# The router's exponential takes its input from SBUF, and a batch's last logits move to the next head pair

## The chip, the cores and the metric

The program runs on one core of one Trainium2 chip. A core has five engines that run side by side and meet only at semaphores: TensorE (PE, matmuls and transposes, results into PSUM), VectorE (DVE), ScalarE (ACT), GpSimd (POOL) and SyncE (SP, which issues most transfers). Each engine takes its instructions strictly in the order of its own list. The metric is the time of one execution on the device in microseconds; a lower number is better.

## The reference

Two parts follow each other. Causal attention with a decay, for 8 batches, 8 heads, 576 positions and a head size of 64:

```python
scores = scale * np.matmul(q, k.transpose(0, 1, 3, 2))
decay = cum[:, :, :, None] - cum[:, :, None, :]      # cum: running sum of log(f)
scores = np.where(causal, -1000000000.0, scores + decay)
attn = softmax(scores)                               # rows divided by their sum + 1e-9
x = (attn @ v) as 4608 rows of 512
```

Then a mixture of experts over these 4608 rows. Each row goes to one of 8 experts, the one with the largest logit, and its result is weighted with that expert's probability:

```python
logits = x @ w_gate                                  # 4608 x 8
expert_idx = np.argmax(logits, axis=1)
probs = np.exp(logits - logits.max(-1, keepdims=True))
probs /= probs.sum(-1, keepdims=True) + 1e-09
gate_w = probs[np.arange(N), expert_idx]
h = np.maximum(xe @ w1[e], 0.0); out[mask] = gate_w[mask, None] * (h @ w2[e])
```

The change touches only how `logits`, `logits - max` and `exp` are scheduled and where they are stored.

## The kernel before

**Attention.** The work goes head pair by head pair: 32 pairs n, four for each batch (p is n modulo 4), each in seven steps i from 0 to 6. In a step, PE computes a group of score tiles of pair n into one of three PSUM banks (pool `ps_s`, L332) and transposes a group of the weights of pair n-1 into one of two banks (`ps_t`, L400, L419, L430). DVE adds the mask and takes the row's extreme in the same instruction (`s_red`, L339, followed by a short read of the accumulator); ACT takes the exponential (L346) and copies most of the transposed tiles to SBUF (L391), DVE the rest (L389). In step 1, PE also does all of attention-times-values of pair n-2 (`av`, L470) into the two banks of pools `ps_v` and `ps_m`, ACT casts keys for pair n+1 (`k_first`, L291) and then copies the two results to SBUF (`av_out`, L479). POOL prepares the operands of later pairs (L249, L287, L296).

**Routing.** When the fourth pair of batch b has gone through `av`, which is step 1 of pair g = 4b+6, the routing of that batch is spread over the following pairs by a table (`r` in `fin_tasks`) of entries (pair after g, step, function). Right behind `av` of pair g stand four small matmuls for the gate (`fin_gate`, L542). In pair g (p = 2) follow a transpose of the output (`fx[0]`, L508) in step 2, the logits of four row blocks (`lg[0]`) in step 3 and of the fifth (`lg[1]`) in step 4: PE transposes (L558), DVE multiplies by the reciprocal row sums (L562), and after the last block DVE adds over the heads (L568). In pair g+1 (p = 3) stand `softmax` and `expert` in step 1, `rank` in step 3; in pair g+2 (p = 0) `gate` and `slot`, and so on. The bank of `lg` is `fin_bank[0]`, which alternates between `ps_v` in even and `ps_m` in odd steps. For the last batch (b = 7) the order is another one, written out in `Moe.finish`.

`softmax` takes the maximum of the logits (L805) and subtracts it (L807, into `w.sh`). `expert` takes the exponential on ACT (L811) and then, on DVE, finds the index of the largest logit (L814 to L824); `rank` counts with six small matmuls on PE (L840, L842) which need the result of L824, and DVE finishes the count (L847 to L856).

**One PSUM bank for the routing.** `c.ps_r` is a single bank of 512 columns that all the routing's small PSUM values share: the logits in columns 0 to 39, `w.sh` in 40 to 79, the one-hot rows, the counts. The framework adds a semaphore wait where two engines use this bank, also where both only read it.

**What sets the order.** Each engine's order is the order of the code, pinned step by step (`InOrder.pin`); nothing reorders it. The framework adds the waits. After the attention the experts follow one by one (L1093 for the first, L1116 for the second matrix), and their first expert's work already begins in the last pairs.

Of the kernel before, what the change touches and what calls it, by code (L numbers as in the profile page):

```python
# [8 lines left out]
F32 = mybir.dt.float32  # L9
# [4 lines left out]
AF = mybir.ActivationFunctionType  # L14
ALU = mybir.AluOpType
# [4 lines left out]
P = 128  # L20
# [61 lines left out]
def psum(pool):  # L82
    return pool.tile([P, 512], F32, name="ps", tag="ps")
# [11 lines left out]
def attention_all(c, tc, qkT, va, vb, f, wgd, x_dram, batch_done, more_consts, extra):  # L95
# [6 lines left out]
    nc = tc.nc  # L102
    V = nc.vector
# [11 lines left out]
    with ExitStack() as st:  # L115
# [5 lines left out]
        ps_s, ps_t, ps_v, ps_m = c.ps_s, c.ps_t, c.ps_v, c.ps_m  # L121
# [4 lines left out]
        def note(r):  # L126

            pe_last[:] = [r.ins]
            return r
# [416 lines left out]
                    ))  # L546
                nc.scalar.copy(gT[:, q0:q1], g[:, 0 : q1 - q0])

        def fin_logits(b, part):
            rinv = rinvs[b]  # L550
            if part == 0:
                lgs[b] = (c.ps_r[:, 0:40].rearrange("p (t e) -> p t e", e=8),
                          sm.tile([P, 5, 8, 8], F32, name="gq", bufs=1))
            lg, gq = lgs[b]
            pg = psum(fin_bank[0])
            tiles = (0, 1, 2, 3) if part == 0 else (4,)
            for i, t in enumerate(tiles):
                note(nc.tensor.transpose(  # L558
                    pg[:, P * i : P * i + P], gT[:, P * t : P * t + P], c.ident
                ))  # L560
            for i, t in enumerate(tiles):
                V.tensor_tensor(  # L562
                    gq[:, t],
                    pg[:, P * i : P * i + P].rearrange("q (h e) -> q e h", e=16)[:, 0:8, :],
                    rinv[:, t, :].unsqueeze(1).to_broadcast([P, 8, 8]), ALU.mult,
                )
            if part == 1:
                V.tensor_reduce(lg, gq, AX.X, ALU.add)  # L568


        fin_bank = [ps_m]

        def fin_tasks(b):

            (softmax, expert, gate, rank, slot, hi, lo, table), after = batch_done(
                b, lambda: lgs[b][0]
            )
            fx = [lambda t=t: fin_x(b, t, b == B - 1 and t > 0) for t in range(5)]  # L580
            lg = [lambda p=p: fin_logits(b, p) for p in range(2)]
            g = NPAIR * b + 6
            if b == B - 1:
                return dict(fx=fx, lg=lg, softmax=softmax, expert=expert, gate=gate,
                            rank=rank, slot=slot, hi=hi, lo=lo, table=table,
                            logits=lambda: fin_gate(b))
            r = [(0, 2, fx[0]), (0, 3, lg[0]), (0, 4, lg[1]), (1, 1, softmax),
                 (1, 1, expert), (1, 3, rank)]
            if b < B - 2:
                r += [(2, 1, gate), (2, 1, slot), (2, 2, fx[1]), (2, 3, fx[2]),  # L590
                      (3, 1, hi), (3, 1, lo), (3, 2, fx[3]), (3, 3, fx[4]), (3, 5, table)]
            else:
                r += [(2, 1, gate), (2, 1, slot), (2, 2, fx[1]), (2, 3, hi), (2, 3, lo),
                      (2, 4, fx[2]), (2, 5, fx[3]), (2, 6, fx[4]), (3, 0, table)]
            for dn, i, f in r + after:
                tasks.setdefault((g + dn, i), []).append(f)
# [47 lines left out]
        for n in range(NP + 2):  # L644
            b, p = divmod(n, NPAIR)
# [84 lines left out]
E = 8  # L730
# [56 lines left out]
def route_stages(c, tc, b, lg_of, last):  # L787

    nc = tc.nc
    V = nc.vector  # L790
    rs = c.rps
    bc = lambda a: a.unsqueeze(2).to_broadcast([P, 5, E])
    flat = lambda a: a.rearrange("p t e -> p (t e)")
    w = Ctx()
    vl = c.vals[:, 5 * b : 5 * b + 5, :]

    part = lambda o, n: c.ps_r[:, o : o + n]
    tokens = lambda o, n: part(o, n * E).rearrange("p (t e) -> p t e", e=E)  # L800

    def softmax():
        lg = lg_of()
        mx = rs.tile([P, 5], F32, name="mx")
        V.tensor_reduce(mx, lg, AX.X, ALU.max)  # L805
        w.sh = tokens(40, 5)
        V.tensor_tensor(w.sh, lg, bc(mx), ALU.subtract)  # L807

    def expert():
        w.ex = rs.tile([P, 5, E], F32, name="ex")  # L810
        nc.scalar.activation(w.ex, w.sh, AF.Exp)  # L811

        cand = rs.tile([P, 5, E], F32, name="cand")
        V.scalar_tensor_tensor(  # L814
            flat(cand), flat(w.sh), 0.0, flat(c.iota5m), ALU.is_ge, ALU.mult
        )
        w.ei = part(128, 5)
        V.tensor_reduce(w.ei, cand, AX.X, ALU.min)
        w.oh = tokens(80, 6)
        V.tensor_tensor(w.oh[:, 0:5], bc(w.ei), c.iota5m, ALU.is_equal)  # L820
        V.memset(w.oh[64:128, 4, :], 0.0)
        V.memset(w.oh[:, 5, :], 0.0)
        w.ohb = rs.tile([P, 6, E], BF16, name="ohb")
        V.tensor_copy(w.ohb, w.oh)  # L824

    def gate():

        gw = part(136, 5)
        V.tensor_reduce(gw, w.ex, AX.X, ALU.add)
        V.tensor_scalar(gw, gw, 1.0e-9, None, ALU.add)  # L830
        V.reciprocal(gw, gw)
        for i in range(3):
            V.tensor_copy(vl[:, :, 3 + i], gw)
            if i < 2:
                V.tensor_tensor(gw, gw, vl[:, :, 3 + i], ALU.subtract)

    def rank():

        w.pr = part(192, 48)
        nc.tensor.matmul(w.pr[:, 0:48], c.trib, flat(w.ohb), start=True, stop=False)  # L840
        for s in range(1, 6):
            nc.tensor.matmul(  # L842
                w.pr[:, 8 * s : 48], c.onesb, flat(w.ohb[:, 0 : 6 - s]),
                start=False, stop=(s == 5),
            )
        rk = rs.tile([P, 6, E], F32, name="rk", bufs=2)
        V.tensor_tensor(rk, w.pr[:, 0:48].rearrange("p (t e) -> p t e", e=E),  # L847
                        c.carry.unsqueeze(1).to_broadcast([P, 6, E]), ALU.add)
        c.carry = rk[:, 5, :]
        V.tensor_tensor(rk[:, 0:5], w.oh[:, 0:5], rk[:, 0:5], ALU.mult)  # L850
        w.r = rs.tile([P, 5], F32, name="r")
        w.rp = part(144, 5)
        for r in (w.r, w.rp):
            V.tensor_reduce(r, rk[:, 0:5], AX.X, ALU.add)

        V.memset(w.ei[64:128, 4:5], -4.0 - E)  # L856

    def slot():
        r, ei = w.r, w.ei
        V.scalar_tensor_tensor(c.key[:, 5 * b : 5 * b + 5], ei, 8192.0, r,  # L860
                               ALU.mult, ALU.add)

        th = rs.tile([P, 5, NST - 1], F32, name="th")
        V.tensor_tensor(
            th, w.rp.unsqueeze(2).to_broadcast([P, 5, NST - 1]),
            c.iotaP[:, 1:NST].unsqueeze(1).to_broadcast([P, 5, NST - 1]), ALU.is_ge,
        )
        hi = rs.tile([P, 5], F32, name="hi")
        V.tensor_reduce(hi, th, AX.X, ALU.add)
        w.lo = part(152, 5)  # L870
        V.scalar_tensor_tensor(w.lo, hi, -float(P), w.rp, ALU.mult, ALU.add)
        w.hi = part(160, 5)
        V.scalar_tensor_tensor(w.hi, ei, float(NST), hi, ALU.mult, ALU.add)

    def onehot_hi():
        eqh = rs.tile([P, 5, NHI], BF16, name="eqh")
        V.tensor_tensor(
            eqh, w.hi.unsqueeze(2).to_broadcast([P, 5, NHI]),
            c.iotah.unsqueeze(1).to_broadcast([P, 5, NHI]), ALU.is_equal,
        )  # L880
        w.R = rs.tile([P, 5, 6, NHI], BF16, name="Rr")
        eng = V if last else nc.gpsimd
        for t in range(5):
            eng.tensor_tensor(
                w.R[:, t], eqh[:, t].unsqueeze(1).to_broadcast([P, 6, NHI]),
                vl[:, t].unsqueeze(2).to_broadcast([P, 6, NHI]), ALU.mult,
            )

    def onehot_lo():
        w.A = rs.tile([P, 5, P], BF16, name="Ar")  # L890
        V.tensor_tensor(w.A, w.lo.unsqueeze(2).to_broadcast([P, 5, P]),
                        c.iota128.unsqueeze(1).to_broadcast([P, 5, P]), ALU.is_equal)

    def table():

        pt = part(256, 6 * NHI)
        for t in range(5):
            nc.tensor.matmul(pt[:, 0 : 6 * NHI], w.A[:, t],
                             w.R[:, t].rearrange("p v h -> p (v h)"),
                             start=(t == 0), stop=(t == 4))  # L900
        tab = c.tab.rearrange("p v h -> p (v h)")
        V.tensor_tensor(tab, tab, pt[:, 0 : 6 * NHI], ALU.add)

    return [softmax, expert, gate, rank, slot, onehot_hi, onehot_lo, table]


# [514 lines left out]
```

## Time and profile before

| | us |
|---|---|
| median of 3 runs | 862.28 (861.4 to 862.44) |
| the profiled execution | 861.09 |
| its span, first to last instruction | 859.3 |
| PE busy in the span | 816.6 (95%) |
| DVE, ACT, POOL busy | 462.9, 432.3, 388.2 |

The profiled execution is 1.19 us shorter than the median, and 1.8 us of it lie outside the span. In the timeline, times count from the start of the span; a row gives the start, the length, the engine, the line, the operation, what it writes and reads, the size and, in square brackets, how long the engine stood idle before it and who ended that. A matmul's row is as long as its way through the array, so rows of PE overlap; how long PE needs for a group is seen from one start to the next.

### The profile page before, as it was taken

To read this page: it belongs to the slowest core of one execution; us is meant where nothing else is said; L and a number is where in the kernel's file an instruction comes from. 1 tells how busy PE (TensorE), PEld (TensorE's weight loads), DVE (VectorE), ACT (ScalarE), POOL (GpSimd) and SP (SyncE) were. 2 spreads that over 40 slices of the span, in tenths; PEclk is the share of its full clock that TensorE was granted. 3 is DMA by queue.
4 is the path that set the end of the run, shared out by engine and by line. 5 is a ranking of instruction groups with operands and counts; after the bars stand their busy time and mean duration, and the time that the engine had idled before them with its cause. 6 is when DMAs were issued, how large, how long until landed. Compare 5 with 4: busy or idle time off the path is not lost. (4 is left out here: it accounts for less than half of the span.)

```text
span 859.3 us, 15386 instructions
## 1 busy us (share of the span) xinstructions
PE 816.6 (95%) x5664; PEld 713.9 (83%) x5664; DVE 462.9 (54%) x1427; ACT 432.3 (50%) x1108; POOL 388.2 (45%) x310
## 2 busy tenths in 40 slices
PE   4899999999999999999999999999999999999992
PEld 3778787878787878788899899898898998988982
DVE  7656767676767778655472544445425444354200
ACT  6888888888888989855221223122122221231210
POOL 7798696969696978651530230312203103101010
PEclk9999999999999999999999999999999999999996
DMA  7997676767676765522651450533415405324000
GB/s 170 223 191 162 163 178 164 183 150 187 152 184 154 176 152 146 175 93 86 191 190 50 147 170 21 189 109 119 149 46 171 143 4 183 104 74 132 1 37 17
DMA packets 39893, 114.65 MB, mean 133 GB/s; under 512 B 6847, under 2 KB 8895, under 8 KB 36104
## 3 DMA queue, kind: packets, MB, share of 16 engines
q1 hardware_dynamic: 32776, 93.70, 42.2%
q0 software_dynamic: 6400, 19.93, 6.4%
q8 instruction: 46, 0.75, 0.4%
q14 instruction: 31, 0.25, 0.1%
q10 hardware_dynamic: 640, 0.01, 0.0%
HBM read 94.07 MB, written 20.55 MB: 133 GB/s over the span
## 5 line engine op out<-in xcount | busy, mean ns | idle before, releaser
L1116 PE MATMUL ps<-w,hh 128*128 128x512 f32 x640 | 199.3, 395 | 0.0
L346 ACT ACTIVATE sc<-sc,nmx 128x512 f32<-128x512 f32 (+4 forms) x288 | 167.3, 582 | 34.7 <-DVE nmx L339 34.2
L1124 POOL DMA_INDIRECT out<-y,si_fast x37 | 42.4, 1146 | 312.1 <-ACT y L1123 283.4
L339 DVE CUSTOM_DVE_ANT_0 sc<-ps,mask 128x512 f32<-128x512 f32 (+4 forms) x288 | 129.2, 479 | 63.7 <-PE ps L332 63.0
L1098 ACT ACTIVATE hh<-ps 128x384 fp32r<-128x384 f32 (+1 forms) x128 | 56.1, 438 | 194.5 <-PE ps L1093 194.5
L1093 PE MATMUL ps<-xa,w 128*128 128x384 f32 x768 | 145.1, 337 | 0.1
L332 PE MATMUL ps<-qk 128*128 128x288 f32 (+4 forms) x384 | 126.9, 361 | 16.0 <-ACT qk L271 10.8
L1099 DVE SCALAR_TENSOR_TENSOR hl<-ps,hh 128x384 fp32r<-128x384 f32 (+1 forms) x128 | 62.4, 489 | 146.2 <-ACT hh L1098 145.0
L1116 PEld LDWEIGHTS ps<-w,hh 128*128 128x128 f32 x640 | 118.2, 188 | 23.6
L1093 PEld LDWEIGHTS ps<-xa,w 128*128 128x128 f32 x768 | 132.7, 188 | 1.4 <-DVE hl L1099 0.2
L1116 PE MATMUL ps<-w,hl 128*128 128x512 f32 x320 | 124.8, 395 | 0.0
L332 PE MATMUL ps<-k,q 68*128 68x288 f32 (+4 forms) x384 | 105.7, 323 | 5.2 <-POOL k L249 3.8
L249 POOL TENSOR_TENSOR k<-raw,qk 64x1152 fp32r<-64x1152 f32 x30 | 79.4, 2647 | 53.7 <-ACT qk L291 49.0
L1093 PE MATMUL ps<-xb,w 128*128 128x256 f32 x768 | 101.8, 283 | 0.0
L1093 PEld LDWEIGHTS ps<-xb,w 128*128 128x128 f32 x768 | 98.9, 189 | 2.8
L470 PE MATMUL ps<-aT,va_t 128*64 128x256 f32 (+3 forms) x896 | 94.6, 354 | 0.0
L1123 ACT ACTIVATE y<-ps,g_fast 128x512 f32<-128x512 f32 x37 | 25.5, 689 | 136.6 <-PE ps L1116 130.7
L391 ACT COPY aT<-ps 128x512 f32<-128x512 f32 (+1 forms) x156 | 83.2, 534 | 14.1 <-PE ps L400 6.8
L332 PEld LDWEIGHTS ps<-qk 128*128 128x128 f32 x384 | 69.6, 195 | 23.6 <-ACT qk L271 10.8
L249 POOL TENSOR_TENSOR qk<-raw,qk 64x1280 fp32r<-64x1280 f32 x30 | 87.8, 2928 | 2.4
L470 PEld LDWEIGHTS ps<-aT,va_t 128*64 128x64 f32 x896 | 58.9, 137 | 29.2 <-issue 6.1
L969 DVE CAST w<-wraw 128x1024 fp32r<-128x1024 f32 x56 | 39.2, 707 | 80.3 <-PE ps L1116 54.3
(161 smaller groups left out, 1133.2 us busy)
## 6 DMA issues: line engine op xcount, KB each, us to landing
raw<-in_qkT SPq DMA_DIRECT2D x58, 608.0 KB
wraw<-in_w SPq DMA_DIRECT2D x63, 512.0 KB
va_t<-in_va SPq DMA_DIRECT2D x32, 256.0 KB
x_dram<-row SPq DMA_DIRECT2D x32, 256.0 KB
raw<-in_qkT SPq DMA_DIRECT2D x6, 320.0 KB
raw<-in_qkT SPq DMA_DIRECT2D x6, 288.0 KB
vb<-in_vb SPq DMA_DIRECT2D x32, 32.0 KB
x_dram<-row SPq DMA_DIRECT2D x8, 128.0 KB
```

The lines of the kernel that those rows point to most:

```text
L249: return eng.tensor_tensor(o, raws[n][p0 : p0 + 64, c0:c1], ops[n][0][p0 : p0 + 64, c0:c1].bitcast(F32), ALU.subtract,)
L332: note(nc.tensor.matmul(out, ql[:, q0 : q0 + P], kl[:, j, k0 : k0 + kw], start=(i == 0), stop=(i == last),))
L339: V.tensor_tensor_reduce(scs[n][:, dst : dst + src.shape[1]], src, m, -0.125, init, ALU.add, ALU.min, nms[n][:, col : col + 1],)
L346: nc.scalar.activation(x, x, AF.Exp, bias=nms[n][:, col : col + 1], scale=-1.0, accum_out=acc)
L391: nc.scalar.copy(dst, src)
L470: c.last_av = note(nc.tensor.matmul(pv[j * HD : (j + 1) * HD, q0 - qa : qb - qa], l, r, start=(blk == 0), stop=(blk == nb - 1),))
L969: V.tensor_copy(w[:, 0], raw)
L1093: c.note(nc.tensor.matmul(ph[:, 0:n], w[:, wi, fs], x[:, xi, kt, :], start=(k == 0), stop=(k == 3 * KT - 1),))
L1098: nc.scalar.activation(hh[:, ft, :], ph[:, 0:n], AF.Relu)
L1099: nc.vector.scalar_tensor_tensor(hl[:, ft, :], ph[:, 0:n], 0.0, hh[:, ft, :].bitcast(F32), ALU.max, ALU.subtract,)
L1116: c.note(nc.tensor.matmul(py, hi_[:, ft, ms], w[:, wi], start=(ft + k == 0), stop=(ft == FT - 1 and k == 2),))
L1124: nc.gpsimd.indirect_dma_start(out=self.out, out_offset=bass.IndirectOffsetOnAxis(ap=si[:, s : s + 1], axis=0), in_=y, in_offset=None, bou ...
```

## The change

There are two edits, in the table of `fin_tasks` and in `softmax`/`expert`.

- `lg[1]`, the logits of a batch's fifth row block, leaves step 4 of pair g and stands in step 0 of pair g+1, and it uses the bank of `ps_m` instead of the one that `fin_bank` names (which is `ps_v` in both steps).
- `softmax` subtracts the maximum a second time, into a new SBUF tile `shs`, and the exponential reads `shs` instead of `w.sh`. DVE's search for the largest logit goes on reading `w.sh`.

The last batch goes through `Moe.finish`, where the place and the bank of `lg[1]` stay as they were; there the second subtraction alone is new.

```diff
-        def fin_logits(b, part):
+        def fin_logits(b, part, bank=None):
...
-            pg = psum(fin_bank[0])
+            pg = psum(bank or fin_bank[0])
...
-            r = [(0, 2, fx[0]), (0, 3, lg[0]), (0, 4, lg[1]), (1, 1, softmax),
+            r = [(0, 2, fx[0]), (0, 3, lg[0]), (1, 0, lambda: fin_logits(b, 1, ps_m)), (1, 1, softmax),
                  (1, 1, expert), (1, 3, rank)]
...
         w.sh = tokens(40, 5)
         V.tensor_tensor(w.sh, lg, bc(mx), ALU.subtract)
 
+        w.shs = rs.tile([P, 5, E], F32, name="shs")
+        V.tensor_tensor(w.shs, lg, bc(mx), ALU.subtract)
+
     def expert():
         w.ex = rs.tile([P, 5, E], F32, name="ex")
-        nc.scalar.activation(w.ex, w.sh, AF.Exp)
+        nc.scalar.activation(w.ex, w.shs, AF.Exp)
```

From L808 on the lines of the changed kernel count three higher (L814 becomes L817, L840 becomes L843).

DVE before, around step 4 of pair g (`sc`, `nmx` are the scores and their row extremes, `pr` the routing's bank, `gq` the logits per head; the bracket names the engine whose semaphore is waited for):

```order
L389 COPY aT<-ps 128x2x2x128 [waits PE_49]
L562 TENSOR_TENSOR gq<-ps,rinv 128x64 [waits PE_49]
L568 TENSOR_REDUCE pr<-gq 128x40 [waits DVE_49]
L339 ISA sc,nmx<-ps,mask 128x288 [waits PE_49]
L339 ISA nmx 128x1
L389 COPY aT<-ps 68x2x64
```

and from `softmax` on, some rows further down:

```order
L805 TENSOR_REDUCE mx<-pr 128x5
L807 TENSOR_TENSOR pr<-pr,mx 128x40 [waits DVE_49]
L814 SCALAR_TENSOR_TENSOR cand<-pr,iota5m 128x40 [waits Activation_49]
L818 TENSOR_REDUCE pr<-cand 128x5 [waits DVE_49]
L820 TENSOR_TENSOR pr<-pr,iota5m 128x40 [waits DVE_49]
```

The search (`cand`) waits for ACT, though it takes nothing from it. The same engine in the changed kernel, from step 0 of pair g+1:

```order
L339 ISA sc,nmx<-ps,mask 128x512 [waits PE_49]
L339 ISA nmx 128x1
L562 TENSOR_TENSOR gq<-ps,rinv 128x64 [waits PE_49]
L568 TENSOR_REDUCE pr<-gq 128x40 [waits DVE_49]
L339 ISA sc,nmx<-ps,mask 128x512 [waits PE_49]
L339 ISA nmx 128x1
L805 TENSOR_REDUCE mx<-pr 128x5 [waits DVE_49]
L807 TENSOR_TENSOR pr<-pr,mx 128x40 [waits DVE_49]
L810 TENSOR_TENSOR shs<-pr,mx 128x40 [waits DVE_49]
L817 SCALAR_TENSOR_TENSOR cand<-pr,iota5m 128x40
L821 TENSOR_REDUCE pr<-cand 128x5 [waits DVE_49]
L823 TENSOR_TENSOR pr<-pr,iota5m 128x40 [waits DVE_49]
```

The two instructions of `lg[1]` now stand behind the reductions of two joint tiles and of step 0, there is one more subtraction (L810), and `cand` has lost its wait for ACT. On ACT the exponential keeps its place and its wait for DVE; only its source is another.

PE in the changed kernel, from step 0 of pair g+1 into its `av`, the transpose of `lg[1]` (L558) now behind the first transposes:

```order
L332 MATMUL ps<-k_1_145,q_1_143 128x512 [waits DMAHW2_49,DMAHW1_49,Pool_49]
L400 MATMUL ps<-ident,sc 128x128 [waits DVE_49]
L400 MATMUL ps<-ident,sc 128x128 x3
L558 MATMUL ps<-ident,gT 128x128
L332 MATMUL ps<-qk_920 128x512 [waits DVE_49,PE_49]
```

and some rows on, the second half of `av`, which writes the bank of `ps_m`:

```order
L470 MATMUL ps<-aT,vb_176 64x64 [waits DMAHW0_49]
L470 MATMUL ps<-aT,vb_176 64x64
L470 MATMUL ps<-aT,va_t 64x320 [waits DVE_49]
L470 MATMUL ps<-aT,va_t 64x320
L470 MATMUL ps<-aT,va_t 64x192 x2
L470 MATMUL ps<-aT,va_t 64x64 x2
```

Before, L558 stood behind the transposes of step 4 of pair g, and the first `64x320` had no wait; now it waits until DVE has read the logits out of that bank (L562).

## The prediction

> **What bounds the kernel now.** I read the waits of the whole span first, then the span cut at the starts of the head pairs, then the timelines of PE, DVE and ACT in one pair. The waits have one entry at the place of the change, DVE's search for the largest logit behind ACT's exponential: 24.5 us in 8 times.
>
> ```profile
> DVE cand L814 <- ACT ex L811: 24.5, 8, 3.5
> ```
>
> DVE is no bound by its busy time, so this matters only if PE waits for DVE later. The cut says so. A row gives the stretch, its length, then busy time of PE, PEld, DVE, ACT and POOL. The first row is a pair with p = 3, where the search and the count (`rank`) stand; the second a pair with p = 1, in which PE has eight more full transposes and five small matmuls (the table):
>
> ```profile
> 128.10:139.85 11.75, 10.50 (x90) 8.36 (x89) 7.42 (x38) 8.90 (x26) 7.89 (x5) 1.00 0.57 134
> 150.40:161.19 10.79, 10.79 (x97) 9.46 (x96) 8.13 (x31) 9.78 (x28) 10.58 (x12) 1.00 0.79 190
> ```
>
> The pair with less work for PE takes 0.96 us longer. PE is the bound in the second pair; in the first it stands still. Where, the starts on PE's timeline tell, p = 3 first, p = 1 as the measure behind it:
>
> ```profile
> 128.65 0.60 PE L400 MATMUL ps<-ident,sc 128*128 128x128 f32 x4
> 129.33 0.47 PE L332 MATMUL ps<-qk 128*128 128x512 f32 x1
> 130.41 1.84 PE L470 MATMUL ps<-aT,va_t 128*64 128x256 f32 x16
> 133.27 0.44 PE L332 MATMUL ps<-qk 128*128 128x384 f32 x1
> 133.91 0.63 PE L400 MATMUL ps<-ident,sc 128*128 128x128 f32 x4
> 134.90 0.62 PE L400 MATMUL ps<-ident,sc 128*128 128x128 f32 x4
> 135.97 0.20 PE L840 MATMUL pr<-ohb,trib 128*128 128x48 bf16 x1 [0.44 <-DVE ohb L824]
> 136.13 0.36 PE L332 MATMUL ps<-qk 128*128 128x256 f32 x1
> 136.85 0.66 PE L419 MATMUL ps<-ident,sc 128*128 128x128 f32 x4
> 138.53 0.60 PE L430 MATMUL ps<-ident,sc 128*128 128x128 f32 x4
> 139.85 0.47 PE L332 MATMUL ps<-qk 128*128 128x512 f32 x1 [0.72 <-DVE nmx L339]
> 141.03 0.47 PE L332 MATMUL ps<-qk 128*128 128x512 f32 x1
> ```
>
> ```profile
> 150.40 0.48 PE L332 MATMUL ps<-qk 128*128 128x512 f32 x1
> 150.95 0.60 PE L400 MATMUL ps<-ident,sc 128*128 128x128 f32 x4
> 151.31 0.48 PE L332 MATMUL ps<-qk 128*128 128x512 f32 x1
> 157.31 0.63 PE L400 MATMUL ps<-ident,sc 128*128 128x128 f32 x4
> 157.77 0.60 PE L508 MATMUL ps<-ident,xT 128*64 128x128 f32 x4
> 158.13 0.37 PE L332 MATMUL ps<-qk 128*128 128x256 f32 x1
> 158.70 0.61 PE L419 MATMUL ps<-ident,sc 128*128 128x128 f32 x4
> ```
>
> Four transposes take 0.36 us to the next scores (150.95 to 151.31) and 0.46 to an operation of another kind (157.31 to 157.77). In p = 3 the same steps take 0.68, 1.07 (134.90 to 135.97) and 1.32 us (138.53 to 139.85): 0.32, 0.61 and 0.96 us of standing still. With the 0.15 by which step 4's scores take longer (136.13 to 136.85 against 158.13 to 158.70) that is 2.04 us. DVE's and ACT's timelines of the same pair show the source:
>
> ```profile
> 127.88 0.22 DVE L562 TENSOR_TENSOR gq<-ps,rinv 128x64 f32<-128x64 f32 x1
> 128.53 0.45 DVE L339 CUSTOM_DVE_ANT_0 sc<-ps,mask 128x288 f32<-128x288 f32 x1
> 129.57 0.69 DVE L339 CUSTOM_DVE_ANT_0 sc<-ps,mask 128x512 f32<-128x512 f32 x1
> 131.03 0.21 DVE L807 TENSOR_TENSOR pr<-pr,mx 128x40 f32<-128x40 f32 x1
> 134.71 0.20 DVE L814 SCALAR_TENSOR_TENSOR cand<-pr,iota5m 128x40 f32<-128x40 f32 x1 [3.47 <-ACT ex L811]
> 135.70 0.21 DVE L824 CAST ohb<-pr 128x48 bf16<-128x48 f32 x1
> 137.91 0.29 DVE L389 COPY aT<-ps 128x128 f32<-128x128 f32 x1 [0.43 <-ACT aT L391]
> ```
>
> ```profile
> 136.42 0.62 ACT L346 ACTIVATE sc<-sc,nmx 128x384 f32<-128x384 f32 x1 [1.37 <-DVE nmx L339]
> 137.42 0.46 ACT L391 COPY aT<-ps 128x384 f32<-128x384 f32 x1
> 137.78 0.62 ACT L346 ACTIVATE sc<-sc,nmx 128x384 f32<-128x384 f32 x1
> ```
>
> The exponential stands on ACT behind the key cast and the copies of `av`'s results, so it comes late, and DVE, whose L807 is done at 131.24, stands behind it for 3.47 us. Step 2's reduction is late by that, ACT waits 1.37 us for it, ACT's copy of step 3 (137.42) is late, DVE's copy of the same bank (137.91) waits for that one, and behind it stand the end of the count and step 4's reduction, which frees the bank that PE needs at 139.85 (its row names L339's `nmx`).
>
> **The change part by part.** *The search no longer waits for ACT.* DVE then goes from L807 (131.03) to the second subtraction at 131.26 and to the search at 131.49, 3.22 us earlier, and the one-hot row (L824) is there at 135.91 - 3.22 = 132.69, before PE reaches the count. The 0.61 us are gone. Step 2's reduction is no longer behind anything on DVE; it waits for PE.
>
> *The second subtraction.* It reads a PSUM operand and a small SBUF operand and writes SBUF, like L562, and has the size of L807 (0.21 us). With L562 as the nearest row of that kind, and free of dependence on what POOL does at the time in 40 instances, I take 0.23 us from start to start:
>
> ```profile
> L562 DVE TENSOR_TENSOR gq<-ps,rinv x40: 211/215/219, 81.5 to 395.6; 128x64 f32<-128x64 f32 x40
> ```
>
> The bounds are 0.2 and 0.25 us. What hides it: DVE is through at 132.69 and has no scores before about 133.8. Without that cover it would cost 0.23 us in each of 7 batches, 1.6 us. The exponential now waits for this subtraction (131.47), which is long done when ACT comes to it; its length changes by nothing that matters, since nobody on DVE waits for it until the next pair.
>
> *The logits of the fifth block.* L562 and L568 leave DVE between 127.88 and 128.53, so 0.65 us come off ahead of the last reductions of pair g, which is why PE's second scores came 0.32 us late (129.33): that goes too. The 0.65 us stand in step 0 now, ahead of step 1's reduction, whose scores PE has by then; that one ends near 130.9, and ACT needs it after 131. On PE, L558 goes from one pair to the next. As its price I take the 0.46 - 0.36 = 0.10 us by which an operation of another kind comes later behind four transposes, with 0 below and above it the 0.36 us of a whole group of four. It falls off pair g and comes onto pair g+1, so the sum does not hang on it. No transfer is moved, and no other queue is passed.
>
> *The new wait of `av`.* PE's 64x320 matmuls now wait for L562. DVE's reduction of step 0 moves from 129.57 to 128.92 and ends 0.61 later (its accumulator is read at its end), so L562 ends near 129.8. PE comes to the matmuls behind the first half of `av`, which starts at 130.19 and takes some 1.8 us: near 132.0. The cover is 2.2 us; behind the wait stands all of PE.
>
> *What is late next.* PE without standing still: first scores 128.10, the second 0.91 later as in p = 1 and 0.10 for L558 (129.11), then the distances of the rows, 130.41 - 129.33 = 1.08 and 133.27 - 130.41 = 2.86: step 2 at 133.05, its transposes 0.64 later at 133.69, done 0.62 later at 134.31. ACT copies them at 134.35, needs 0.36 until the exponential (137.42 to 137.78): 134.71 in place of 136.42. That is 1.71 us earlier, and this shift passes through ACT's copy of step 3 and DVE's copy (137.91, now 136.20) to the reduction of step 4 and to PE at 139.85, now 138.14. PE itself, without the 2.04 and with the 0.10, would be there at 137.91, so 0.23 us of its standing still remain: DVE's tail, the copy, the count and the reduction in a row, still sets the end. Pair g+1 shrinks by 1.71 to 10.04 us, pair g by 0.10. The next pair keeps its length, because the same tail comes before it. 1.81 us for each of the six batches with a whole next pair: 10.9 us.
>
> *The seventh batch.* The last pair of scores (batch 6) has the same wait, and there PE stands still longer:
>
> ```profile
> 357.34 0.62 PE L400 MATMUL ps<-ident,sc 128*128 128x128 f32 x4
> 359.74 0.62 ACT L346 ACTIVATE sc<-sc,nmx 128x384 f32<-128x384 f32 x1 [1.26 <-DVE nmx L339]
> 361.71 0.29 DVE L389 COPY aT<-ps 128x128 f32<-128x128 f32 x1 [0.91 <-ACT aT L391]
> 364.76 1.00 PE L400 MATMUL ps<-ident,sc 128*128 128x128 f32 x4 [1.94 <-DVE aT L389]
> ```
>
> By the same walk PE's transposes of step 2 come 0.3 us earlier, are done at 357.66, and the exponential starts at 358.07 in place of 359.74: 1.67 us, which run through 361.71 to 364.76. With pair g's 0.10 these are 1.8 us. The eighth batch's wait is the small rest of the 24.5 us, in a stretch where PE has the experts' work, and counts nothing.
>
> *The clock.* Behind that pause the granted clock falls to half for 3.4 us; the column before the last two is the clock:
>
> ```profile
> 136.40:139.80 3.40, 2.73 (x21) 2.27 (x20) 2.86 (x18) 2.86 (x10) 3.32 (x3) 1.00 0.03 8
> 361.60:365.00 3.40, 1.46 (x12) 1.22 (x11) 3.18 (x15) 2.28 (x10) 0.00 (x0) 0.99 0.12 46
> 365.00:368.40 3.40, 3.40 (x20) 2.51 (x20) 1.40 (x6) 2.69 (x7) 0.00 (x0) 0.51 0.03 7
> ```
>
> A stretch in which PE was busy for 1.46 of 3.40 us preceded the fall, one with 2.73 did not cause it. DVE frees PE 1.67 us earlier, PE itself is there some 0.8 us earlier (0.3 at the second scores, the rest at the count), so about 1.1 us of pause and 2.3 busy remain, nearer to the first row. I count the fall as gone. Half of 3.4 us is 1.7 us of lost work, but the copies and splits behind which PE stands there are not faster, so I take 0.4, with 0 and 1.7 as bounds. [...] The trace has the fall directly behind the pause, and I go by it.
>
> The sum is 10.9 + 1.8 + 0.4 = 13.1 us. The profiled execution of 861.09 us (859.3 of span and 1.8 around it) becomes 848.0; the median, 1.19 above it, becomes 862.28 - 13.1 = 849.2 us. Behind 400 us PE has no pause to speak of, so nothing gives the gain back.
>
> **The rivals.** *The tail keeps its place (15%).* Only what comes ahead of the count goes, 0.32 and 0.61, and the end of p = 3 stays as late because ACT is the one that is late there. For: ACT is busy 8.90 us of that pair, the most after PE. Against: it waited 1.37 us for DVE. 7 times 0.93 is 6.5, so 855.8 us.
>
> *All of PE's pauses go (10%).* 2.04 us and the 0.27 that p = 0 loses in the same way at its second scores (139.85 to 141.03 is 1.18, where p = 1 has 0.91), in six batches; 1.94 + 0.3 + 0.1 in the seventh; and the clock's 1.7: 17.9 us, 844.4. Against: the walk leaves 0.23 us in each p = 3, and the 0.27 behind it.
>
> *DVE's wait is hidden (3%).* Then nothing changes: 862 us. PE's own rows name DVE as what ended its pauses, which speaks against it.
>
> *Slower: `av` waits for the logits (3%).* If DVE came to L562 late, PE would stand at the 64x320 matmuls with everything behind it. It decides from 2.2 us of lateness on, and from about 4.0 (2.2 and the 1.81 of gain) the kernel is slower. Were the 3.47 us to stand ahead of L562 and the rest of the gain lost, it would cost 1.27 us in 7 batches, 8.9 us: 871. DVE waits for nothing of ACT between 127.88 and 131.03.
>
> **How the numbers follow.** The forecast, with 69%, has 849.2 us. The range from 844.9 to 855.2 reaches towards the second rival and the first as far as partial forms of them go, and leaves out their ends and the last two. Faster by over 0.2% (1.7 us, about what runs of this kernel can tell) are the forecast and the first two rivals, 94%; 3% each for no change and slower.
>
> **What would show it.** The entry of `cand` behind the exponential is gone from the waits, p = 3 takes about 10.0 us instead of 11.75, p = 0 and p = 1 stay at 10.55 and 10.8, p = 2 loses 0.1; PE's pause at the count is gone, and the one at the end of the pair is 0.2 us instead of 0.96. No row shows 64x320 behind L562. Wrong would be a pair p = 3 above 10.8, a `cand` that still waits, or a clock at half behind the last pair of scores, which alone costs 0.4.

## The result and the profile after

The changed kernel takes 848.72 us (median of 4 runs, 847.09 to 849.95) against 862.31 before; the ratio is 0.9843, with a 95% interval from 0.9823 to 0.9864. 849.2 was forecast. The profiled execution takes 849.63 us, 847.9 of them span.

DVE's search for the largest logit, now L817, no longer waits for anybody: its entry under the waits is gone, and its own line has no idle time before it. What is left near it is a single wait of ACT for the second subtraction, of the last batch; before, ACT waited there in the same way for the first one (2.3 us). From the view of that line and from the waits of the whole span, after:

```profile
L817 DVE SCALAR_TENSOR_TENSOR cand<-pr,iota5m x8: 189/190/191, 88.6 to 385.2; 128x40 f32<-128x40 f32 x8
```

```profile
ACT ex L814 <- DVE shs L810: 2.5, 1, 2.5
```

The span cut at the starts of the head pairs, with the columns as before: p = 3, p = 0, p = 1 and p = 2.

```profile
127.96:138.03 10.07, 10.00 (x91) 8.49 (x90) 7.82 (x40) 9.05 (x27) 6.79 (x5) 1.00 0.68 155
138.03:148.58 10.55, 10.54 (x90) 8.95 (x90) 9.38 (x42) 9.86 (x29) 8.02 (x5) 1.00 0.77 188
148.58:159.39 10.81, 10.81 (x98) 9.50 (x96) 8.29 (x31) 9.78 (x28) 10.60 (x12) 1.00 0.79 192
159.39:170.76 11.37, 11.37 (x109) 9.40 (x106) 6.74 (x31) 10.08 (x28) 10.03 (x6) 1.00 0.70 164
```

The pair with the search and the count has gone from 11.75 to 10.07 us. The pairs with p = 0 and p = 1 are as they were. PE's timeline of p = 3, to be read against that of before:

```profile
128.51 0.60 PE L400 MATMUL ps<-ident,sc 128*128 128x128 f32 x4
128.95 0.27 PE L558 MATMUL ps<-ident,gT 128*128 128x128 f32 x1
128.98 0.48 PE L332 MATMUL ps<-qk 128*128 128x512 f32 x1
...
133.56 0.63 PE L400 MATMUL ps<-ident,sc 128*128 128x128 f32 x4
...
134.56 0.62 PE L400 MATMUL ps<-ident,sc 128*128 128x128 f32 x4
135.02 0.19 PE L843 MATMUL pr<-ohb,trib 128*128 128x48 bf16 x1
...
135.17 0.37 PE L332 MATMUL ps<-qk 128*128 128x256 f32 x1
...
135.74 0.60 PE L419 MATMUL ps<-ident,sc 128*128 128x128 f32 x4
...
137.36 0.60 PE L430 MATMUL ps<-ident,sc 128*128 128x128 f32 x4
138.03 0.47 PE L332 MATMUL ps<-qk 128*128 128x512 f32 x1
```

The second scores follow 0.47 us behind the first transposes, with the moved L558 between (0.68 before, without it). The count follows 0.46 us behind the transposes of step 3 (1.07 before), the next pair 0.67 us behind the last transposes (1.32 before, 0.36 where nothing waits). Step 4's scores take 0.57 us (135.17 to 135.74), as in p = 1, and no longer 0.72. DVE in the same pair, and two rows of ACT:

```profile
131.00 0.21 DVE L807 TENSOR_TENSOR pr<-pr,mx 128x40 f32<-128x40 f32 x1
131.25 0.20 DVE L810 TENSOR_TENSOR shs<-pr,mx 128x40 f32<-128x40 f32 x1
131.36 0.19 DVE L817 SCALAR_TENSOR_TENSOR cand<-pr,iota5m 128x40 f32<-128x40 f32 x1
...
132.35 0.21 DVE L827 CAST ohb<-pr 128x48 bf16<-128x48 f32 x1
133.76 0.56 DVE L339 CUSTOM_DVE_ANT_0 sc<-ps,mask 128x384 f32<-128x384 f32 x1 [1.21 <-PE ps L332]
...
136.09 0.29 DVE L389 COPY aT<-ps 128x128 f32<-128x128 f32 x1 [0.38 <-ACT aT L391]
136.30 0.20 DVE L850 TENSOR_TENSOR rk<-pr,rk 128x48 f32<-128x48 f32 x1
...
137.11 0.42 DVE L339 CUSTOM_DVE_ANT_0 sc<-ps,mask 128x256 f32<-128x256 f32 x1
```

```profile
133.78 0.25 ACT L814 ACTIVATE ex<-shs 128x40 f32<-128x40 f32 x1
...
134.60 0.62 ACT L346 ACTIVATE sc<-sc,nmx 128x384 f32<-128x384 f32 x1
```

The exponential keeps its place on ACT, 5.82 us after the start of the pair (6.36 before), but DVE is through at 132.56 and waits for PE for 1.21 us. The order of the tail is the old one: copy of step 3, end of the count, reduction of step 4.

Where the time went, in three stretches of the span: up to the start of pair 5, the last one ahead of the first routing; from there to the start of pair 31, the last with scores; and from there to the end. Before:

```profile
0.00:62.13 62.13, 44.80 (x317) 38.10 (x317) 39.09 (x131) 47.37 (x119) 51.02 (x60) 1.00 0.88 198
62.13:351.44 289.31, 281.64 (x2445) 235.24 (x2444) 205.92 (x893) 252.81 (x699) 229.69 (x156) 1.00 0.69 164
351.44:859.30 507.86, 490.13 (x2908) 440.52 (x2906) 217.83 (x405) 132.14 (x292) 107.53 (x96) 0.98 0.33 108
```

and after:

```profile
0.00:64.13 64.13, 48.09 (x317) 40.40 (x317) 39.43 (x131) 47.89 (x121) 49.73 (x59) 0.95 0.86 193
64.13:342.05 277.92, 277.49 (x2446) 235.55 (x2444) 207.14 (x899) 253.04 (x698) 231.31 (x157) 1.00 0.72 171
342.05:847.90 505.85, 487.99 (x2909) 439.45 (x2907) 218.56 (x408) 131.97 (x292) 107.77 (x96) 0.99 0.34 108
```

The middle gives 11.39 us and the end 2.01, together 13.40; the start, in which no changed instruction stands, takes 2.00 us more in this execution, at a mean clock of 0.95 instead of 1.00 (the last section). So the two profiled executions differ by 11.46 us, and without their starts by 13.40, close to the 13.6 between the medians.

### The profile page after: what moved, and what is told of

Read it like the earlier page. It is cut to its first block, busy times and chain, and to the rows that moved or that the text cites. A ratio compares the mean times of both kernels' runs of the same rounds, so it can differ in the third digit from the quotient of the medians.

```text
span 847.9 us, 15394 instructions
## 1 busy us (share of the span) xinstructions
PE 813.6 (96%) x5664; PEld 715.4 (84%) x5664; DVE 465.1 (55%) x1435; ACT 432.9 (51%) x1108; POOL 388.8 (46%) x310
```

## The experiments

The theory was the one of the prediction: DVE's wait at the search makes its tail late, the tail frees the bank that PE waits for, and the place of the fifth block's logits costs the second scores. Each kernel below was timed in three rounds beside the kernel before. The length of the pairs with p = 3 and p = 0 is read from PE's timeline as above, as the median over the steady batches.

**One edit alone.** The exponential reads from SBUF and the logits stay:

```diff
-            r = [(0, 2, fx[0]), (0, 3, lg[0]), (1, 0, lambda: fin_logits(b, 1, ps_m)), (1, 1, softmax),
+            r = [(0, 2, fx[0]), (0, 3, lg[0]), (0, 4, lg[1]), (1, 1, softmax),
```

> Only the exponential reads from SBUF; the fifth block's logits stay in step 4 of pair g. Theory (DVE's wait at the search made the tail of p = 3 late; the logits' place costs the second scores): the search has no wait for ACT, the pause at the count is gone, but PE's second scores in p = 3 stay 0.3 us late, so step 2's exponential starts 1.5 us earlier instead of 1.7; p = 3 takes 10.25 us, p = 2 stays at 11.49, and six batches with 1.5, 1.5 for the seventh and 0.4 for the clock give about 851.5 us. Rival (the logits' place is the larger part): p = 3 above 11 us, 857 or more.

850.27 us, ratio 0.9863 (0.9846 to 0.9879). p = 3 takes 10.31 us, p = 2 11.48, the count follows 0.46 us behind its transposes, and PE's second scores come 0.70 us behind the first ones, as late as before:

```profile
127.28 0.60 PE L400 MATMUL ps<-ident,sc 128*128 128x128 f32 x4
127.98 0.47 PE L332 MATMUL ps<-qk 128*128 128x512 f32 x1
```

The theory holds, the rival does not.

And the logits move, while the exponential goes on reading the bank:

```diff
-        w.shs = rs.tile([P, 5, E], F32, name="shs")
-        V.tensor_tensor(w.shs, lg, bc(mx), ALU.subtract)
...
-        nc.scalar.activation(w.ex, w.shs, AF.Exp)
+        nc.scalar.activation(w.ex, w.sh, AF.Exp)
```

> Only the fifth block's logits move; the exponential still reads the PSUM bank. Theory: the search still waits for ACT, some 20 us in 8 times; the second scores' 0.32 us are gone, ACT gets its joint tile 0.65 us earlier and so reaches the exponential up to 0.65 us earlier, p = 3 takes 11.1 us, p = 2 11.38, about 857 us. Rival (the logits' place is the larger part): p = 3 near 10.1 us, 849 to 851.

857.36 us, ratio 0.9943 (0.9927 to 0.996); p = 3 takes 11.22 us, p = 2 11.38. The waits of DVE from 70 us on, and PE's way to the count:

```profile
DVE cand L814 <- ACT ex L811: 20.0, 8, 2.8
```

```profile
134.52 0.62 PE L400 MATMUL ps<-ident,sc 128*128 128x128 f32 x4
135.28 0.20 PE L840 MATMUL pr<-ohb,trib 128*128 128x48 bf16 x1
```

The wait shrinks from 24.5 to 20.0 us, as expected: ACT's exponential now stands 5.82 us after the start of the pair. The second scores are on time (0.47 us), of the 0.61 us at the count 0.30 are left (0.76 us against 0.46), and the pause at the end of the pair keeps its length (1.33 us). Against 862.43 us alone, the edits are worth 12.2 and 5.1 us; together 13.6, measured against 862.31. They overlap: an earlier ACT shortens the same wait that the first edit removes.

**The wait without SBUF.** The logits moved, no second subtraction, and the exponential put behind the search in the program:

```diff
     def expert():
-        w.ex = rs.tile([P, 5, E], F32, name="ex")
-        nc.scalar.activation(w.ex, w.shs, AF.Exp)
...
         V.tensor_copy(w.ohb, w.oh)
+        w.ex = rs.tile([P, 5, E], F32, name="ex")
+        nc.scalar.activation(w.ex, w.sh, AF.Exp)
```

> The logits moved as in the change, no second subtraction; the exponential reads the PSUM bank, but stands behind the search in the program, so that the bank's wait falls on ACT (for the end of the search) and not on DVE. Theory (it is the order of two readers of one bank, not where the input lies): as the change, 848.7 within 1.5 us, p = 3 at 10.07 us, the search without a wait. Rival (reading from SBUF itself is worth something, or ACT now waits for the search): p = 3 above 10.3 us, 851 or more.

848.01 us, ratio 0.9832 (0.9816 to 0.9849), p = 3 at 10.06 us, and no wait of the search. So what the change removes is an order between two readers of one bank, in which the early one stood behind the late one; where the exponential's input lies is of no weight by itself here. One more instruction was not needed for that.

**The second subtraction, five times.**

```diff
-        V.tensor_tensor(w.shs, lg, bc(mx), ALU.subtract)
+        for _ in range(5):
+            V.tensor_tensor(w.shs, lg, bc(mx), ALU.subtract)
```

> The change with the second subtraction five times over, the same result each time: 4 more on DVE, each 0.11 to 0.23 us from start to start, 0.45 to 0.9 us in each batch. Theory (DVE stands idle for 1.21 us behind the one-hot row and the count comes later still): p = 3 stays at 10.07 us, the time at 848.7 within 1 us. Rival (the subtraction is on the path): p = 3 grows by what is added, up to 0.9 us, 3 to 6 us in all.

848.05 us, ratio 0.9837 (0.9817 to 0.9858), p = 3 at 10.07 us. DVE's timeline of that kernel:

```profile
131.75 1.13 DVE L811 TENSOR_TENSOR shs<-pr,mx 128x40 f32<-128x40 f32 x5
...
134.26 0.56 DVE L339 CUSTOM_DVE_ANT_0 sc<-ps,mask 128x384 f32<-128x384 f32 x1 [0.28 <-PE ps L332]
```

The added 0.9 us come out of the 1.21 us of idle time, of which 0.28 remain. The cover is real, and it has this size.

**The bank of the logits.** `ps_v` instead of `ps_m`, so that the wait falls on the first half of attention-times-values:

```diff
-            r = [(0, 2, fx[0]), (0, 3, lg[0]), (1, 0, lambda: fin_logits(b, 1, ps_m)), (1, 1, softmax),
+            r = [(0, 2, fx[0]), (0, 3, lg[0]), (1, 0, lg[1]), (1, 1, softmax),
```

> The change with the fifth block's logits in the bank of ps_v instead of ps_m, so that the first half of attention-times-values waits for them, not the second. Theory: L562 is done at 129.73 in the changed kernel and the first half starts at 130.06 without a wait, a cover of 0.3 us; p = 3 stays at 10.07 us or grows by no more than 0.1, 848.7 us. Rival (the wait behind the logits decides the time, and ps_m was what kept it away): p = 3 at 10.3 us or more, 850.5 or more.

849.16 us, ratio 0.9854 (0.9834 to 0.9875), p = 3 at 10.07 us, and PE has no wait between 70 and 340 us that the profile lists. Even a cover of 0.3 us is enough; the choice of the bank costs nothing and gains nothing that can be told.

**The rest of the pause: the count later.** The change with `rank` in step 6:

```diff
-                 (1, 1, expert), (1, 3, rank)]
+                 (1, 1, expert), (1, 6, rank)]
```

> The change with the count (rank) in step 6 of pair g+1 instead of step 3. Theory (what is left of PE's pauses comes from DVE's tail, copy, count and reduction in a row): the 0.3 us at the end of p = 3 and the 0.27 us at the second scores of p = 0 go, p = 3 takes 9.85 us and p = 0 10.28, the last pause behind batch 6 shrinks by up to 0.8, together 3 to 4 us: about 845.5 us. Rival (the tail hangs on ACT's copy of step 3 alone): p = 3 and p = 0 as in the change, 848.7.

846.42 us, ratio 0.9814 (0.9798 to 0.9831). Pairs p = 3 and p = 0 of that kernel:

```profile
127.33:137.09 9.76, 9.76 (x91) 8.46 (x90) 7.62 (x36) 9.26 (x28) 6.46 (x5) 1.00 0.71 160
137.09:147.64 10.55, 10.51 (x97) 8.98 (x92) 9.57 (x46) 9.55 (x28) 8.32 (x5) 1.00 0.77 190
```

Half of the expectation came in. p = 3 lost its pause. In p = 0 the second scores are on time, but the pair is as long as before, and one step later PE stands still instead. ACT's and PE's timelines there:

```profile
139.88 0.72 ACT L346 ACTIVATE sc<-sc,nmx 128x512 f32<-128x512 f32 x1 [0.43 <-DVE nmx L339]
...
142.83 0.69 ACT L479 COPY xT<-ps 128x256 f32<-128x256 f32 x2
```

```profile
142.58 0.62 PE L400 MATMUL ps<-ident,sc 128*128 128x128 f32 x4
143.25 0.66 PE L508 MATMUL ps<-ident,xT 128*128 128x128 f32 x4
143.66 0.42 PE L332 MATMUL ps<-qk 128*128 128x384 f32 x1
```

The end of the count now stands ahead of step 0's reduction, ACT waits 0.43 us for that one, its copies of `av`'s results (142.83) stand as far behind the start of the pair as in the change (5.74 us, 5.72 there) although PE is earlier now, and the transposes of the output (L508), which use the same bank, come 0.67 us behind L400 instead of 0.46.

**The count earlier.** `rank` in step 1, right behind the search, where DVE is idle:

```diff
-                 (1, 1, expert), (1, 3, rank)]
+                 (1, 1, expert), (1, 1, rank)]
```

> The change with the count (rank) right behind the search, in step 1 of pair g+1, where DVE stands idle for 1.2 us. Theory (the count in DVE's tail makes p = 3 and the second scores of p = 0 late; in step 6 it makes the first reduction of p = 0 late, ACT with it, and PE waits for ACT's copies there): p = 3 at 9.75 to 9.9 us, p = 0 at 10.3 instead of 10.55, 844.5 to 845.5 us. Rival (p = 0 is bound by ACT wherever the count stands): p = 0 stays at 10.55 and the time is as with the count in step 6, 846.4. Other rival (the count waits for the one-hot row at the end of attention-times-values): p = 3 at 10.1 or more.

844.54 us, ratio 0.9789 (0.9765 to 0.9814). The same two pairs:

```profile
127.92:137.59 9.67, 9.67 (x91) 8.38 (x90) 8.10 (x40) 9.02 (x28) 6.37 (x5) 1.00 0.71 161
137.59:147.87 10.28, 10.28 (x92) 9.00 (x91) 9.11 (x42) 9.78 (x28) 8.44 (x5) 1.00 0.80 191
```

Both are full now: PE goes from the last transposes of p = 3 to the next scores, and from the first transposes of p = 0 to its second scores, in 0.36 us each, the distance where nothing waits. The remaining pauses came from the count in DVE's tail, and both rivals fall.

**SBUF once more, with the count early.** The count in step 1, and the exponential behind the search as in the kernel without the second subtraction, whose edit of `expert` stands above:

```diff
-                 (1, 1, expert), (1, 3, rank)]
+                 (1, 1, expert), (1, 1, rank)]
...
-        nc.scalar.activation(w.ex, w.shs, AF.Exp)
...
         V.tensor_copy(w.ohb, w.oh)
+        w.ex = rs.tile([P, 5, E], F32, name="ex")
+        nc.scalar.activation(w.ex, w.sh, AF.Exp)
```

> The count in step 1 as in rank_early, and the search ahead of the exponential, which reads the PSUM bank, without the second subtraction. Theory: one DVE instruction less where DVE has room, so as rank_early within 0.5 us, unless the exponential on ACT now waits for the count's matmuls, which write the same bank behind it: then PE waits for ACT at the count, 0.5 to 1 us in each p = 3, and the time is 848 to 851.

852.65 us, ratio 0.9894 (0.987 to 0.9917): 8.1 us slower than with the SBUF copy, a little worse than expected, with p = 3 at 10.77 us. PE's waits from 70 to 340 us, and the place on PE and on ACT:

```profile
PE pr L839 <- ACT ex L823: 6.4, 6, 1.1
```

```profile
133.84 0.18 PE L839 MATMUL pr<-ohb,trib 128*128 128x48 bf16 x1 [1.07 <-ACT ex L823]
```

```profile
133.57 0.22 ACT L823 ACTIVATE ex<-pr 128x40 f32<-128x40 f32 x1
```

The exponential's read of the bank now stands between the search and the count's matmuls, and PE waits for the late ACT. With the count in step 1, reading from SBUF is worth 8.1 us over this order; with the count in step 3 it was worth nothing over a better order. The third order, with the exponential behind the count's matmuls, was not run.

**Both side by side.** The change and the version with the early count, both without any further edit, on one chip:

> The changed kernel itself once more, on the chip of the next one: 848.7 us within 1.5, p = 3 at 10.07 and p = 0 at 10.54 us. Where the clock is halved at the start of the program is left to chance, and moves an execution by up to 2 us.

> The count in step 1 beside the change on one chip: per batch 10.07 + 10.54 - 9.67 - 10.28 = 0.66 us, four us in six batches, and a little more behind batch 6: 844.5 us, 4 to 4.5 below the change. If the two differ by less than 2 us, the pair lengths do not add up to the time.

848.94 us (848.03 to 850.43) and 844.04 us (842.09 to 844.16), ratios to before 0.9848 (0.9828 to 0.9869) and 0.9791 (0.9775 to 0.9807). The version with the early count beats both kernels: 4.9 us below the change and 18.3 below the kernel before. The pairs account for 4.0 us of the 4.9 (0.67 us in each of six batches), and PE's pause behind the last scores for 0.6 more (0.95 to 0.36 us).

## Why the prediction was right

*What bounds the kernel.* PE's starts, not its busy time, showed where it stands still, and the chain behind that (exponential, search, reduction of step 2, ACT, copies, count, reduction of step 4) is borne out at both ends by runs: the first edit alone removes the pause at the count and leaves the second scores late, the second alone brings the second scores on time and leaves half of the pause at the count and all of the one at the end, and moving the count takes away what the change leaves of the latter. The links between, from ACT to the copies, are read from the waits in the rows.

*The pair p = 3.* 10.04 us were worked out, 10.07 measured; 0.10 us for L558 in the pair ahead, 0.12 measured (11.49 to 11.37). That pair before:

```profile
161.19:172.68 11.49, 11.49 (x109) 9.51 (x108) 7.06 (x32) 10.10 (x28) 9.86 (x6) 1.00 0.70 164
```

The step that carried this was the question what is late next: that DVE's copy waits for ACT's copy of step 3, so that the gain is ACT's 1.71 us and not DVE's 3.22. ACT's exponential of step 2 starts 6.64 us after the pair (127.96 to 134.60), 8.32 before (128.10 to 136.42): 1.68 us earlier.

*What remained.* 0.23 us of PE's pause at the end of the pair were to stay. Of the 0.67 us from the last transposes to the next scores 0.31 are pause. The tail as its cause was argued there; the two kernels with the count moved show it.

*The second subtraction* was priced at 0.23 us. From L807 to the search it is 0.36 us, where 0.46 was reckoned: the search has nothing to wait for behind it and follows after 0.11 us. The cover was put at a little over 1 us; it is 1.21.

*The seventh batch and the clock.* 1.67 and 0.4 us were forecast. That the fall of the clock would go was an estimate from PE's busy time ahead of it (1.46 of 3.40 us); what decides on a fall no run shows (the last section). PE's first transposes behind the last scores, before and after, with the start of that pair:

```profile
351.44 0.48 PE L332 MATMUL ps<-qk 128*128 128x512 f32 x1
```

```profile
342.05 0.48 PE L332 MATMUL ps<-qk 128*128 128x512 f32 x1
...
353.72 0.66 PE L400 MATMUL ps<-ident,sc 128*128 128x128 f32 x4 [0.95 <-DVE aT L389]
```

From the start of the pair that is 11.67 us instead of 13.32 (364.76 - 351.44), 1.65 us earlier, and the pause is 0.95 instead of 1.94 us. The clock does not fall there any more (1.00 behind the pause, below), and the stretch to the end is 2.01 us shorter, which leaves 0.36 us for the clock and for whatever else differs there; no run separates the two.

*The rivals.* The tail did not keep its place (p = 3 would have lost 0.93 us, it lost 1.68). Not all of PE's pauses went. PE never waited for the logits' bank: L562 ended at 129.73 us, and the matmuls behind it started at 131.85, 2.12 us later, where 2.2 were reckoned. The sum, 13.1 us, is 0.5 us short of the 13.6 between the medians, which is inside what single runs differ by; against the 13.40 of the profile's middle and end it is 0.3 short. The middle gave 11.39 where 11.0 were reckoned (10.9, and 0.10 for the pair ahead of the seventh batch's last one). In it are two pairs outside the walk: pair 5 is 0.25 us shorter (9.65 to 9.40) and pair 24 0.34 (10.88 to 10.54). Without these the middle is 10.80, so the walk's own part came out 0.2 us below its sum, and 0.59 us of the gain is not the walk's. In the kernel with the search first both pairs have their old length, though its pairs with p = 3 are as short as the change's; what moves them is open, and that they raised the total here is luck.

## What to carry to other kernels

A wait between two engines that only read the same PSUM bank shows up in the profile like a dependency (here 24.5 us in 8 times): look whether the waiting instruction takes anything from the one it waits for, and if not, put the early reader first in the program or give the late one a copy elsewhere. The order was enough as long as the bank's next writer came later than the late reader; with the count in step 1 it was not, and the copy was worth 8.1 us. How much that gains is not the length of the wait, here 3.47 us, but the shift of the next instruction behind which the bound engine really stands, here 1.7 us; follow it hop by hop until a second input of a hop comes later. What was left then came from work that stood in a full stretch of DVE, while DVE had been idle for 1.21 us earlier in the same pair, and moving it there was worth another 4.9 us.

## What the runs showed of the hardware beyond that

At the end of the scores the granted clock stayed at full, as forecast. Not foreseen was a fall near the start, behind a pause of PE of 2.86 us. In the profile of after (the column before the last two is the clock; the third row begins with the pause of 0.95 us at the end of the scores):

```profile
38.74:42.15 3.41, 0.83 (x7) 0.52 (x5) 1.58 (x6) 2.24 (x7) 3.41 (x2) 1.00 1.14 253
42.15:48.98 6.83, 6.55 (x29) 4.44 (x31) 1.40 (x4) 3.63 (x7) 6.30 (x5) 0.50 1.03 206
352.76:356.17 3.41, 2.27 (x21) 1.75 (x22) 2.60 (x9) 2.70 (x7) 0.00 (x0) 1.00 0.03 7
```

The length of the pause does not decide this alone. In the kernel before, the clock did not fall at that place of the start, behind 2.60 us:

```profile
38.90:42.30 3.40, 0.81 (x5) 0.50 (x4) 1.32 (x6) 1.98 (x7) 3.40 (x3) 1.00 1.10 237
42.05 0.50 PE L332 MATMUL ps<-k,q 68*128 68x512 f32 x1 [2.60 <-POOL k L249]
42.40 0.60 PE L400 MATMUL ps<-ident,sc 128*128 128x128 f32 x4
42.75 0.48 PE L332 MATMUL ps<-qk 128*128 128x512 f32 x1
```

At the end of the scores, in the same execution, it fell for 3.4 us behind 1.94 us (0.51 from 365.00 to 368.40). The kernel with only the logits moved has a pause of 1.9 us there, and a fall behind it:

```profile
358.20:361.50 3.30, 1.35 (x13) 1.12 (x11) 3.15 (x14) 2.17 (x10) 0.00 (x0) 1.00 0.17 64
361.50:364.90 3.40, 3.35 (x19) 2.08 (x19) 1.44 (x4) 2.69 (x7) 0.00 (x0) 0.50 0.02 7
```

Nor does PE's busy time in the 3.3 to 3.4 us ahead decide it alone, from which the forecast took that the fall would go: falls followed 0.83, 1.35 and 1.46 us of it, and none followed 0.81. What does decide is open; no kernel was built to test it.

Whether the 2.0 us of the start come from this fall alone was not tested by itself. The start of pair 5 comes at 62.13 us in the kernel before, where the column shows no fall before it, and at 64.13 us in the changed kernel, behind the 6.83 us at half; but the pauses ahead of that place differ as well (2.60 and 2.86 us).
